# One pool of buffers for attention and experts, and an expert's first weights loaded ahead of the last batch

## The chip, the cores and the metric

The kernel runs on one core of a Trainium2 chip. The metric is the time of one execution on the device in microseconds (us). TensorE (PE) multiplies matrices, VectorE (DVE) and ScalarE (ACT) work on what it leaves in PSUM and on data in SBUF, GpSimd (POOL) copies and issues the indirect transfers, SyncE (SP) issues the plain transfers.

## What is computed

Linear attention without a softmax, with a normalised output, and behind it a mixture of eight experts, of which each token takes the one with the highest score:

```python
kv  = einsum('bhsd,bhse->bhde', k, v)          # b, h = 8, 8; s = 576; d = 64
out = einsum('bhsd,bhde->bhse', q, kv)
out = out / sqrt(mean(out * out, -1) + 1e-6) * g_norm
x   = out, as [4608 tokens, 512]
expert = argmax(x @ w_gate)                    # 8 experts
p      = softmax(x @ w_gate)[expert]
y[token] = p * (relu(x[token] @ w1[expert]) @ w2[expert])   # 512 -> 1024 -> 512
```

Inputs and output are fp32. A token's expert depends on the data, so rows have to be sorted by expert while the kernel runs.

## The kernel before

**Attention** goes in 36 steps of 128 tokens (the loop at L704). In step s TensorE multiplies the turned queries with K^T V of their batch (`x_mm`, L358), turns the queries of step s + 2 (`x_qt`, L342), and works on K^T V of a coming batch (`kv_mm`, L291; `kv_copy`, `kv_t`, `kv_gate`, L305 to L326). ScalarE squares the result (L389) and makes the reciprocal root (L398, L400), VectorE sums (L394) and writes scaled rows `xg` (L408), from which routing (`Route`) finds each row's expert and rank. GpSimd scatters each block of 128 rows into a scratch in DRAM, sorted by expert (L591). What else happens in a step hangs in three lists, `mid`, `late` and `last`: `at(last, 21, f)` puts f behind the work of step 21.

**Weights** are loaded in fp32 and cast to fp16. `stage1` and `stage2` (L146, L154) issue a 2 MB load of W1 and one of W2 on SP's queue; `half1(engine, kk)` (L173) casts a quarter of W1, on ScalarE (L178) or VectorE (L180), `half2` (L184) a quarter of W2. For expert 0 both loads are hung at step 21, behind the load of batch 7's k, v and q (hung at step 20), and W1's quarters are cast at steps 27 to 30, by ScalarE and VectorE in turn.

**The first three tiles of experts 0 and 1** (`Early`, j0 and j1) are worked on out of attention's pools. j1's three products with W2 are at L784 to L790: `two` is the product (L505), `done` scales it into `ys` (L512) and issues its store (`put`, L214).

**The experts' stage** has pools of its own, opened at L793 when attention's are closed, and nine jobs: the rest of experts 0 and 1 (two tiles of 128 rows each), experts 2 to 7 (five tiles each) and one tile of left-over rows. A job is:

- `flip` (L855): four transposes turn a tile of 128 rows into the PSUM tile `xp`, VectorE copies it to `xt` (L868) and makes the row numbers (L208, `place_rows`). The flips of job n + 1 stand between the blocks of job n.
- `one` (L873): a block. Four matmuls make 128 of the 1024 hidden values for the job's columns (256, or 320 in each of two halves, or 128) in the PSUM tile `hp`, and ScalarE's ReLU writes them to `ht` (L888). A job has 8 blocks, or 16 where it has two halves.
- `two` (L892): eight matmuls make the output rows of a tile in `yp`; VectorE scales them into `ys` (L900) and GpSimd stores them (L214).

[...]the stage gives two to `xp`, three to `hp` and three to `yp`, each bank a tile of its own. Between the blocks VectorE casts W1 of the next job (L180), between the products ScalarE casts W2 (L192), and GpSimd gathers the rows of the job after next (L197, `next_row`). The five gathers for expert 2 and the first two flips of job 0 stand ahead of the loop (L944 to L947). In job 2, behind the second product, VectorE makes the table of left-over rows (`left_over_table`, L798 to L844).

The order on every engine is the written one within a `manual_schedule` (all five engines are under it); there are two of them, one for attention and one for the experts' stage. A tile framework places tiles: a pool hands out `bufs` buffers for each tag in turn, and a new tile of a tag waits for those who used the buffer before; it adds the semaphores.

Of the kernel before, what the change touches and what calls it, by code (L numbers as in the profile page):

```python
# [11 lines left out]
F32 = mybir.dt.float32  # L12
F16 = mybir.dt.float16
# [15 lines left out]
def kernel(  # L29
# [16 lines left out]
    E = 8  # L46
# [181 lines left out]
    with (  # L228
        tc.manual_schedule(engines=by_hand),
        tc.tile_pool(name="pattn", bufs=1) as PA,  # L230
        tc.tile_pool(name="psattn", bufs=1, space=bass.MemoryType.PSUM) as PSA,
    ):
# [374 lines left out]
        def at(where, s, fn, *args):  # L607
            where[s].append(lambda: fn(*args))
# [53 lines left out]
        at(last, 21, W[0].stage1)  # L662
        at(last, 21, W[0].stage2)
        at(last, 30, W[1].stage_in, PA)
        for kk in range(4):
            at(last, 27 + kk, W[0].half1, nc.vector if kk % 2 else nc.scalar, kk)
# [117 lines left out]
        yp0 = PSA.tile([128, D], F32, tag="qtp", bufs=1, name="yp")  # L784
        j1.two(0, yp0)
        j1.done(0, yp0)
        yp = PSA.tile([128, 2, D], F32, tag="kvp", bufs=1, name="yp")
        for t in (1, 2):
            j1.two(t, yp[:, t - 1, :])
            j1.done(t, yp[:, t - 1, :])  # L790


    with (  # L793
        tc.tile_pool(name="pffn", bufs=1) as PF,
        tc.tile_pool(name="psffn", bufs=1, space=bass.MemoryType.PSUM) as PSF,
    ):

        def left_over_table():  # L798

            ovr = PF.tile([128, 8], F32, tag="ovr")  # L800
            nc.vector.tensor_sub(ovr, cnt, dlt)
            nc.vector.tensor_scalar(ovr, ovr, float(CAP), 0.0, op0=ALU.subtract, op1=ALU.max)
            thr = PF.tile([128, 8, 32], F32, tag="thr")
# [4 lines left out]
            ov = PF.tile([128, 8], F32, tag="ov")  # L808
            nc.vector.reduce_sum(ov, thr, axis=AXX)
            oi = PF.tile([128, 8], F32, tag="oi")  # L810
            zero8 = PF.tile([128, 8], F32, tag="zero8")
            nc.vector.memset(zero8, 0.0)
            nc.vector.tensor_tensor_scan(oi, ov, zero8, 0.0, op0=ALU.add, op1=ALU.add)
            cm = PF.tile([128, 32, 8], F32, tag="thr")
            nc.vector.tensor_tensor(cm, _bc(oi, 1, 32), _bc(tcol, 2, 8), op=ALU.is_le)
            te = PF.tile([128, 32], F32, tag="te")
            nc.vector.reduce_sum(te, cm, axis=AXX)
            nc.vector.tensor_tensor(cm, cm, _bc(ov, 1, 32), op=ALU.mult)
            tk = PF.tile([128, 32], F32, tag="tk")
# [3 lines left out]
            e8 = PF.tile([128, 8], F32, tag="e8")  # L823
            nc.vector.tensor_scalar(e8, eoff, 1.0 / N, None, op0=ALU.mult)
            nc.vector.tensor_tensor(cm, _bc(te, 2, 8), _bc(e8, 1, 32), op=ALU.is_equal)
            cd = PF.tile([128, 32, 8], F32, tag="cd")
            nc.vector.tensor_tensor(cd, cm, _bc(dlt, 1, 32), op=ALU.mult)
            td = PF.tile([128, 32], F32, tag="td")
# [16 lines left out]

        class Job:


            def __init__(self, xe, w, okm, bgm, views):
                self.xe, self.w, self.okm, self.bgm, self.views = xe, w, okm, bgm, views  # L850
                self.nt = nt = len(xe)
                self.cols = nt * 128
                self.halves = 2 if self.cols > 512 else 1

            def flip(self, t):  # L855

                nt, xe = self.nt, self.xe
                if t == 0:
                    self.xt = PF.tile(
                        [128, 4, nt * 128], F16, tag=f"xt{nt}", bufs=2, name="xt"  # L860
                    )
                    self.idx = PF.tile([128, nt], I32, tag=f"idx{nt}", bufs=3, name="idx")
                xp = PSF.tile([128, 4, 128], F16, tag="xp", bufs=2, name="xp")
                for c in range(4):
                    nc.tensor.transpose(  # L865
                        xp[:, c, :], xe[t][:, c * 128:(c + 1) * 128], ident16
                    )
                nc.vector.tensor_copy(self.xt[:, :, t * 128:(t + 1) * 128], xp)  # L868
                place_rows(
                    self.idx[:, t:t + 1], xe[t], self.okm[:, t:t + 1], self.bgm[:, t:t + 1]  # L870
                )

            def one(self, ws, f):  # L873
                if ws == 0 and f == 0:
                    self.ht = PF.tile(
                        [128, 8, self.cols], F16, tag=f"ht{self.nt}", bufs=2, name="ht"
                    )
                wd = self.cols // self.halves
                hp = PSF.tile([128, wd], F32, tag="hp", bufs=3, name="hp")
                for kk in range(4):  # L880
                    nc.tensor.matmul(  # L881
                        hp,
                        self.w.w1[:, kk, f * 128:(f + 1) * 128],
                        self.xt[:, kk, ws * wd:(ws + 1) * wd],
                        start=(kk == 0),
                        stop=(kk == 3),
                    )
                nc.scalar.activation(  # L888
                    self.ht[:, f, ws * wd:(ws + 1) * wd], hp, ACTF.Relu
                )  # L890

            def two(self, t):  # L892
                yp = PSF.tile([128, D], F32, tag="yp", bufs=3, name="yp")
                for f in range(8):
                    nc.tensor.matmul(  # L895
                        yp, self.ht[:, f, t * 128:(t + 1) * 128], self.w.w2[:, f, :],
                        start=(f == 0), stop=(f == 7),
                    )
                ys = PF.tile([128, D], F32, tag="ys", bufs=8, name="ys")
# [5 lines left out]
        def left_over(t, t0, view):  # L905
# [5 lines left out]
            okm = PF.tile([128, 1], F32, tag="okm", bufs=2, name="okm")  # L911
            nc.vector.tensor_tensor(okm, pcol, nvf[:, bass.ds(t, 1)], op=ALU.is_lt)
            bgm = PF.tile([128, 1], F32, tag="bgm", bufs=2, name="bgm")
            nc.vector.tensor_scalar(bgm, okm, -BIG, BIG, op0=ALU.mult, op1=ALU.add)
            gi = PF.tile([128, 1], I32, tag="gi", bufs=2, name="gi")
# [7 lines left out]
        with tc.manual_schedule(engines=by_hand):  # L923
            jobs = []
            for n, e in enumerate(order):
                if e == "left":
                    jobs.append(None)
                    continue
                t0 = AT if n < 2 else 0
                x0 = 2 * AT + 2 * n if n < 2 else (10, 0, 5)[(n - 2) % 3]  # L930
                jobs.append(Job(
                    xe_bufs[x0:x0 + CT - t0], W[n], valid[:, e, t0:CT], bigm[:, e, t0:CT],
                    out_views[e * CT + t0:(e + 1) * CT],
                ))

            tick2 = PF.tile([128, 1], F16, tag="tick2")

            def next_row(n, t, job, ws, f):

                c = ws * (job.cols // job.halves)  # L940
                nc.gpsimd.tensor_copy(tick2, job.ht[:, f, c:c + 1])  # L941
                gather(jobs[n].xe[t], rowi[:, order[n], t:t + 1])

            for t in range(CT):  # L944
                gather(jobs[2].xe[t], rowi[:, 2, t:t + 1])
            for t in range(2):
                jobs[0].flip(t)  # L947

            for n in range(len(order)):
                job = jobs[n]  # L950
                if n == 4:
                    jobs[E] = left_over(0, 3 * CT, out_views[E * CT])
                    W[E] = jobs[E].w
                nxt = jobs[n + 1] if n + 1 < len(order) else None
                flips = list(range(nxt.nt)) if nxt is not None else []
                coming = list(range(CT)) if 0 < n < len(order) - 3 else []
                for ws in range(job.halves):
                    for f in range(8):
                        job.one(ws, f)
                        step = 8 * ws + f  # L960
                        if coming and (step % 3 == 0 if n > 1 else f < 5):
                            next_row(n + 2, coming.pop(0), job, ws, f)
                        if ws == job.halves - 1 and f >= 2 and flips:
                            nxt.flip(flips.pop(0))
                        if n > 0 and ws == 0 and f % 2 == 1 and nxt is not None:
                            W[n + 1].half1(nc.vector, f // 2)
                            if f == 7 and n + 2 < len(order):
                                W[n + 2].stage1()
                for kk in range(max(job.nt, 4)):
                    if kk < job.nt:  # L970
                        job.two(kk)
                    if n > 0 and kk < 4 and nxt is not None:
                        W[n + 1].half2(kk)
                        if kk == 3 and n + 2 < len(order):
                            W[n + 2].stage2()
                    if n == 2 and kk == 1:
                        left_over_table()

        nov = nc.values_load(tabi[0:1, 1, 7:8], min_val=0, max_val=NOV)
        with tc.If(nov > 1):  # L980
            with tc.For_i(1, nov) as t:
                job = left_over(t, 3 * CT, out_views[E * CT + 1])
                job.w.stage1()
                job.w.stage2()
                for kk in range(4):
                    job.w.half1(nc.vector, kk)
                    job.w.half2(kk)
                job.flip(0)
                for f in range(8):
                    job.one(0, f)  # L990
                job.two(0)
# [28 lines left out]
```

## Time and profile before

| | us |
|---|---|
| median of 3 runs | 304.49 (304.31 to 304.61) |
| the profiled execution | 330.63 |
| its span, first to last instruction | 328.7 |
| TensorE busy | 276.4 (84%) |
| ScalarE busy | 165.8 (50%) |
| VectorE busy | 157.9 (48%) |
| GpSimd busy | 164.3 (50%) |
| mean granted clock of TensorE | 0.935 of full |

Times in the profile come from one execution with the profiler on, which took 26.1 us more than the median. A row of the timeline is: start, duration, engine, line, operation, output and input with their shapes, how often, and in brackets how long the engine had been idle before it and what ended that. A row of the groups is: line, engine, operation, how often | busy us, mean ns of one | idle us before it, and what ended most of it. "issue" is a wait whose end the profile doesn't show. TensorE's matmuls are pipelined, and their ends are modelled.

### The profile page before, as it was taken

To read this page: it belongs to the slowest core of one execution; us is meant where nothing else is said; L and a number is where in the kernel's file an instruction comes from. 1 tells how busy PE (TensorE), PEld (TensorE's weight loads), DVE (VectorE), ACT (ScalarE), POOL (GpSimd) and SP (SyncE) were. 2 spreads that over 40 slices of the span, in tenths; PEclk is the share of its full clock that TensorE was granted. 3 is DMA by queue.
4 is the path that set the end of the run, shared out by engine and by line. 5 is a ranking of instruction groups with operands and counts; after the bars stand their busy time and mean duration, and the time that the engine had idled before them with its cause. 6 is when DMAs were issued, how large, how long until landed. Compare 5 with 4: busy or idle time off the path is not lost. (4 is left out here: it accounts for less than half of the span.)

```text
span 328.7 us, 7210 instructions
## 1 busy us (share of the span) xinstructions
PE 276.4 (84%) x2832; PEld 191.5 (58%) x2832; DVE 157.9 (48%) x424; ACT 165.8 (50%) x353; POOL 164.3 (50%) x238
## 2 busy tenths in 40 slices
PE   8897989979996967258952999799979999999992
PEld 3586877868885856224521665456446474665651
DVE  0034856844784747524321280787453354546130
ACT  1245766643764656427800356455434466473831
POOL 9511253764365663742773088327685484305051
PEclk9999999985999898769995899999997999999999
DMA  7999878949599767320695029997779597987330
GB/s 283 373 391 389 323 259 313 397 121 394 169 401 398 299 205 277 99 76 26 223 379 221 2 82 350 390 352 272 302 257 402 154 368 290 312 322 254 150 123 33
DMA packets 34883, 85.73 MB, mean 261 GB/s; under 512 B 3868, under 2 KB 4125, under 8 KB 34848
## 3 DMA queue, kind: packets, MB, share of 16 engines
q1 hardware_dynamic: 26592, 65.10, 54.9%
q0 software_dynamic: 6976, 18.96, 15.8%
q10 hardware_dynamic: 1280, 1.20, 1.1%
q8 instruction: 23, 0.38, 0.5%
q14 instruction: 12, 0.10, 0.1%
HBM read 71.71 MB, written 15.50 MB: 265 GB/s over the span
## 5 line engine op out<-in xcount | busy, mean ns | idle before, releaser
L888 ACT ACTIVATE ht<-hp 128x320 f16<-128x320 f32 (+2 forms) x120 | 49.1, 419 | 81.2 <-PE hp L881 70.4
L881 PE MATMUL hp<-xt,w1e 128*128 128x320 f16 (+2 forms) x480 | 72.2, 299 | 11.8 <-DVE xt L868 5.9
L214 POOL DMA_INDIRECT out_dram<-ys,idx x41 | 42.7, 1042 | 71.3 <-DVE ys L900 61.7
L881 PEld LDWEIGHTS <-w1e 128*128 128x128 f16 x480 | 45.7, 100 | 29.0 <-issue 7.4
L895 PE MATMUL yp<-w2e,ht 128*128 128x512 f16 x280 | 61.9, 379 | 0.0
L368 PE MATMUL op<-kvs,qts 128*128 128x144 f32 (+1 forms) x320 | 50.3, 315 | 3.2 <-DVE xg L408 1.9
L591 POOL DMA_INDIRECT xs_scratch<-xg,sli x36 | 35.4, 983 | 22.8 <-issue 22.2
L895 PEld LDWEIGHTS <-ht 128*128 128x128 f16 x280 | 27.3, 98 | 31.4
L368 PEld LDWEIGHTS op<-kvs,qts 128*128 128x128 f32 (+1 forms) x320 | 41.3, 193 | 6.8 <-DVE xg L408 2.3
L900 DVE TENSOR_SCALAR ys<-yp,xe 128x512 f32<-128x512 f32 x35 | 26.0, 750 | 39.9 <-PE yp L895 38.7
L197 POOL DMA_INDIRECT xe<-xs_scratch,rowi x34 | 35.7, 1049 | 9.4 <-issue 6.0
L394 DVE TENSOR_REDUCE ms<-sq 128x8 f32<-128x512 f32 x36 | 24.6, 684 | 22.0 <-ACT sq L389 18.4
L389 ACT ACTIVATE sq<-op 128x512 f32<-128x512 f32 x36 | 21.5, 596 | 25.6 <-PE op L368 22.6
L192 ACT CAST w2e<-ws 128x1024 f16<-128x1024 f32 x32 | 31.2, 1041 | 1.5 <-DMA ws<-in_moe_w_dram 1.5
L868 DVE COPY xt<-xp 128x512 f16<-128x512 f16 x35 | 14.7, 421 | 34.4 <-PE xp L865 21.1
L346 PE MATMUL qtp<-cf,qp 128*128 128x128 f32 x144 | 24.2, 293 | 1.5 <-POOL qp L282 1.5
L299 PE MATMUL kvp<-v,k 64*64 64x64 f32 x1152 | 24.4, 227 | 1.3 <-DMA v<-in_v_dram 0.7
L180 DVE TENSOR_SCALAR w1e<-ws,g 128x1024 f16<-128x1024 f32 x31 | 21.9, 755 | 6.8 <-DMA ws<-in_moe_w_dram 6.8
L408 DVE TENSOR_TENSOR xg<-op,rinv 128x512 f16<-128x512 f32 x36 | 24.5, 681 | 0.0
L299 PEld LDWEIGHTS kvp<-v,k 64*64 64x64 f32 x1152 | 20.3, 138 | 7.0 <-issue 7.0
L353 ACT COPY qts<-qtp 128x512 f32<-128x512 f32 x36 | 21.1, 585 | 6.4 <-PE qtp L346 6.3
L282 POOL COPY qp<-q 128x512 f32<-128x512 f32 x32 | 19.6, 626 | 9.3 <-DMA q<-in_q_dram 9.2
(115 smaller groups left out, 275.9 us busy)
## 6 DMA issues: line engine op xcount, KB each, us to landing
ws<-in_moe_w_dram SPq DMA_DIRECT2D x16, 2048.0 KB
q<-in_q_dram SPq DMA_DIRECT2D x8, 1152.0 KB
k<-in_k_dram SPq DMA_DIRECT2D x7, 1152.0 KB
v<-in_v_dram SPq DMA_DIRECT2D x7, 1152.0 KB
ws<-in_moe_w_dram SPq DMA_DIRECT2D x4, 1024.0 KB
k<-in_k_dram SPq DMA_DIRECT2D x2, 576.0 KB
v<-in_v_dram ACTq DMA_DIRECT2D x2, 576.0 KB
out_dram<-ys,idx POOLq DMA_INDIRECT x41
```

The lines of the kernel that those rows point to most:

```text
L192: copy(self.w2[:, 2 * kk:2 * kk + 2, :], self.s2[:, 2 * kk:2 * kk + 2, :])
L197: return nc.gpsimd.indirect_dma_start(out=xe.bitcast(I32), out_offset=None, in_=xs.ap() if src is None else src, in_offset=IndirectOffsetO ...
L214: nc.gpsimd.indirect_dma_start(out=view, out_offset=IndirectOffsetOnAxis(ap=idx, axis=0), in_=ys, in_offset=None, bounds_check=N - 1, oob_ ...
L299: nc.tensor.matmul(kvst[b][64 * ip:64 * ip + 64, c, 64 * i2:64 * i2 + 64], ld["k", b][ps, i, cs], ld["v", b][ps, i, cs], start=(j == 0), s ...
L368: nc.tensor.matmul(op[ts, c, 144 * i2:144 * i2 + 144], qts[s][:, 2 * i2 + c, ts], kvs[:, 2 * c + i2, :], start=True, stop=True,)
L394: nc.vector.reduce_sum(ms, sq, axis=AXX)
L408: nc.vector.tensor_tensor(xg[:, r, 0:512].rearrange("p (i h c n) -> p c i h n", c=2, i=2, h=2), ox, _bc(r4, 4, 64), op=ALU.mult,)
L591: put_xs = nc.gpsimd.indirect_dma_start(out=xs_views[9 * self.P + self.g0 + t], out_offset=IndirectOffsetOnAxis(ap=self.sli[:, t:t + 1], a ...
L881: nc.tensor.matmul(hp, self.w.w1[:, kk, f * 128:(f + 1) * 128], self.xt[:, kk, ws * wd:(ws + 1) * wd], start=(kk == 0), stop=(kk == 3),)
L888: nc.scalar.activation(self.ht[:, f, ws * wd:(ws + 1) * wd], hp, ACTF.Relu)
L895: nc.tensor.matmul(yp, self.ht[:, f, t * 128:(t + 1) * 128], self.w.w2[:, f, :], start=(f == 0), stop=(f == 7),)
L900: nc.vector.tensor_scalar(ys, yp, self.xe[t][:, 514:516].bitcast(F32), None, op0=ALU.mult)
```

## The change

Attention's pools, SBUF (`PA`) and PSUM (`PSA`), stay open to the end, and the experts' stage takes its buffers from them by attention's tags, in one `manual_schedule`:

- PSUM: `xp` becomes half of a tile of two banks (tag kvp, one buffer), for two flips in a row; `hp` becomes half of a tile of two banks (tag op, two buffers), for two blocks in a row; `yp` takes two tiles of one bank in turn (qtp, misc).
- SBUF: `xt` takes the buffers of k, `ht` is split into two tiles of four blocks in those of v and q, `ys` goes round seven buffers (five of qp, two of sq) where it had eight.
- j1's three products use the same two `yp` tiles, and the first two flips of job 0 stand ahead of the third. The five gathers for expert 2 stand behind j1's stores.
- Expert 0's W1 load is hung at step 19, which is ahead of the load of batch 7 on SP's queue; its four casts are all ScalarE's, at steps 22, 24, 26 and 28.

```diff
-    with (
-        tc.manual_schedule(engines=by_hand),
-        tc.tile_pool(name="pattn", bufs=1) as PA,
-        tc.tile_pool(name="psattn", bufs=1, space=bass.MemoryType.PSUM) as PSA,
-    ):
+    PA = ctx.enter_context(tc.tile_pool(name="pa", bufs=1))
+    PSA = ctx.enter_context(tc.tile_pool(name="psa", bufs=1, space=bass.MemoryType.PSUM))
+
+    with tc.manual_schedule(engines=by_hand):
...
-        at(last, 21, W[0].stage1)
+        at(last, 19, W[0].stage1)
         at(last, 21, W[0].stage2)
         at(last, 30, W[1].stage_in, PA)
         for kk in range(4):
-            at(last, 27 + kk, W[0].half1, nc.vector if kk % 2 else nc.scalar, kk)
+            at(last, 22 + 2 * kk, W[0].half1, nc.scalar, kk)
...
-        yp0 = PSA.tile([128, D], F32, tag="qtp", bufs=1, name="yp")
-        j1.two(0, yp0)
-        j1.done(0, yp0)
-        yp = PSA.tile([128, 2, D], F32, tag="kvp", bufs=1, name="yp")
-        for t in (1, 2):
-            j1.two(t, yp[:, t - 1, :])
-            j1.done(t, yp[:, t - 1, :])
-    with (
-        tc.tile_pool(name="pffn", bufs=1) as PF,
-        tc.tile_pool(name="psffn", bufs=1, space=bass.MemoryType.PSUM) as PSF,
-    ):
...
+        banks = ["qtp", "misc"]
+        spare = ["qp", "sq", "qp", "qp", "sq", "qp", "qp"]
...
             def flip(self, t):
-                    self.xt = PF.tile(
-                        [128, 4, nt * 128], F16, tag=f"xt{nt}", bufs=2, name="xt"
-                    )
+                    self.xt = PA.tile([128, 4, nt * 128], F16, tag="k", bufs=2, name="xt")
-                xp = PSF.tile([128, 4, 128], F16, tag="xp", bufs=2, name="xp")
+                if t % 2 == 0:
+                    self.xp = PSA.tile([128, 2, 8, 128], F16, tag="kvp", bufs=1, name="xp")
+                xp = self.xp[:, t % 2, 0:4, :]
...
             def one(self, ws, f):
-                if ws == 0 and f == 0:
-                    self.ht = PF.tile(
-                        [128, 8, self.cols], F16, tag=f"ht{self.nt}", bufs=2, name="ht"
-                    )
+                if ws == 0 and f % 4 == 0:
+                    self.ht.append(PA.tile(
+                        [128, 4, self.cols], F16, tag="vq"[f // 4], bufs=2 + f // 4,
+                        name="ht",
+                    ))
-                hp = PSF.tile([128, wd], F32, tag="hp", bufs=3, name="hp")
+                if f % 2 == 0:
+                    self.hp = PSA.tile([128, 2, 512], F32, tag="op", bufs=2, name="hp")
+                hp = self.hp[:, f % 2, 0:wd]
...
             def two(self, t):
-                yp = PSF.tile([128, D], F32, tag="yp", bufs=3, name="yp")
+                banks.reverse()
+                yp = PSA.tile([128, D], F32, tag=banks[0], bufs=1, name="yp")
...
-                ys = PF.tile([128, D], F32, tag="ys", bufs=8, name="ys")
+                spare.append(spare.pop(0))
+                ys = PA.tile(
+                    [128, D], F32, tag=spare[0], bufs=5 if spare[0] == "qp" else 2, name="ys"
+                )
...
-            for t in range(CT):
-                gather(jobs[2].xe[t], rowi[:, 2, t:t + 1])
-            for t in range(2):
-                jobs[0].flip(t)
+        for t in range(AT):
+            if t == 2:
+                for u in range(2):
+                    jobs[0].flip(u)
+            banks.reverse()
+            yp = PSA.tile([128, D], F32, tag=banks[0], bufs=1, name="yp")
+            j1.two(t, yp)
+            j1.done(t, yp)
+        for t in range(CT):
+            gather(jobs[2].xe[t], rowi[:, 2, t:t + 1])
```

The table of left-over rows and the job of a left-over tile take their small tiles from the same pool; what they compute is the same.

## The prediction

> **What bounds the kernel now.** I read the groups of instructions first, then the timeline at three places: where attention's buffers hand over to the experts' (155 to 185 us), inside one expert late in the run (286 to 309), and around the table of left-over rows (210 to 226); last, steps 22 to 32 of attention.
>
> The groups say who paces the experts:
>
> ```profile
> L888 ACT ACTIVATE ht<-hp 128x320 f16<-128x320 f32 (+2 forms) x120 | 49.1, 419 | 81.2 <-PE hp L881 70.4
> L881 PE MATMUL hp<-xt,w1e 128*128 128x320 f16 (+2 forms) x480 | 72.2, 299 | 11.8 <-DVE xt L868 5.9
> ```
>
> ScalarE waited 70.4 us for TensorE in front of its ReLUs, TensorE almost nothing. TensorE is the bound of the experts' stage. Now the handover:
>
> ```profile
> 168.00 0.75 DVE L512 TENSOR_SCALAR ys<-yp,xe 128x512 f32<-128x512 f32 x1 [2.01 <-PE yp L505]
> ...
> 168.81 1.89 PE L505 MATMUL yp<-w2e,early 128*128 128x512 f16 x8 [1.88 <-issue]
> ...
> 178.78 0.42 DVE L868 COPY xt<-xp 128x512 f16<-128x512 f16 x1 [5.68 <-DMA out_dram<-ys,idx]
> ...
> 179.72 2.74 PE L881 MATMUL hp<-xt,w1e 128*128 128x256 f16 x12 [5.91 <-DVE xt L868]
> ```
>
> Two waits are seen. The first copy into the new pool (L868) waits until the last store of expert 1 from attention's pool has landed (issued by GpSimd at 175.12; in the chain of waits its landing takes 3.03 us). TensorE stands until 179.72. And the third product of expert 1 (168.81) starts 0.06 us after VectorE has read the second (168.00 + 0.75 = 168.75): they lie in two halves of one tile, yp [128, 2, 512] (L787), each a bank of its own, and still the later write waits for the read of the other half. So the program's dependencies here go by the tile, not by the half. Keep this in mind.
>
> Inside an expert:
>
> ```profile
> 288.49 0.71 PE L881 MATMUL hp<-xt,w1e 128*128 128x320 f16 x4
> ...
> 289.24 0.44 ACT L888 ACTIVATE ht<-hp 128x320 f16<-128x320 f32 x1 [0.33 <-PE hp L881]
> ...
> 300.74 6.14 PE L881 MATMUL hp<-xt,w1e 128*128 128x320 f16 x44
> 301.56 5.79 ACT L888 ACTIVATE ht<-hp 128x320 f16<-128x320 f32 x11 [5.05 <-PE hp L881]
> ```
>
> Eleven blocks of four matmuls without a gap: weight loads of 6.02 us for them, 0.546 us a block. Its ReLU starts 0.75 us after the block's first matmul and takes 0.44. With three hp tiles (L879) nobody waits for it.
>
> **What the Trainium skill says.** "TensorE: Matmul & The Clock Gate", section "Single matmul latency": warm, (398 + N)/2.4 ns, which is 299 ns for N = 320. The row of L881 has 299 ns on average: agreed; so a result is complete some 0.2 us after the next matmul could have started, and 0.546 + 0.2 is the 0.75 above. The same page, section "The HAM clock gate": after an idle window of about 3.4 us the clock goes to half. The trace agrees: granted clock 0.50 in 175 to 180 and 0.62 in 180 to 185, behind the handover; it also fell to 0.5 after a stretch of 3.41 us (245.24 to 248.65) with TensorE busy for 1.51, and did not after one with 2.04 (204.28 to 207.69). "PSUM — Partial Sum Buffer", section "PSUM bank collisions raise a hardware error": what must be kept apart is a bank and quadrant. The two halves of a pair are different banks, so the chip would not need the wait seen at 168.81; the program makes it.
>
> **The change part by part.** The profiled execution took 330.63 us (span 328.7), the median of the runs shown is 304.49: 26.1 less. All terms are sums in the profiled execution's microseconds, and I carry the difference to the median unscaled.
>
> *1. One pool: the handover goes.* In the built program after, the last product of expert 1 stands behind the two flips of the next job and in a tile of its own, so neither the 0.06-after-the-read wait nor the wait for the stores is left. On GpSimd's queue the five gathers for expert 2 (L197, about 1.31 us apart) now stand behind expert 1's three stores, and not among them. TensorE then goes on: two products until about 167.1, eight transposes (L865, x8: 0.67), the third product (1.73), to 169.5; the copies follow the read that ends at 168.75, two of 0.42 and an idx of 0.21 between, so about 169.8. Against 179.72: **-9.9**. What is late next would be the gathers for expert 2: stores at 165.9, 167.7 and about 170.2, gathers to about 177.9, landed by about 181; first needed by a flip at about 181. Covered, 0 to +1.
>
> *2. Blocks in pairs (hp, two blocks to a tile).* In the built program the first matmul of every second block waits for a ScalarE semaphore, and its value is reached by the ReLU of the first block of the same tile. It is the wait by tile from above, now 60 times. For 320 columns: ReLU starts at 0.75, ends at 1.19, 0.05 to TensorE (as at 243.99 to 244.03), so the second block starts 1.24 after the first and not 0.546: **+0.70 a pair** (1.79 against 1.09). For 256 columns: 189.09 to 189.73 is 0.64, +0.39 +0.05 = 1.08 against 0.44: +0.64. Where a flip (four transposes, 0.22) stands between the two blocks, it uses 0.22 of it: three pairs in a job whose successor has five tiles.
> Jobs 4, 5, 6: 8 x 0.70 - 0.66 = 4.94 each, 14.8. Job 7 (one flip): 5.4. Job 0: 3.97 without any wait (8 blocks of 0.44, two flips), +2.56 -0.22 = 6.3, against the 5.9 it took at half clock behind the handover: +0.4. Job 1: 4.63 + 2.56 - 0.66 = 6.5 against 5.5: +1.0. Job 2: it took 13.36 (198.06 to 211.42) where 9.8 is due, since its flips waited behind VectorE's W1 cast, which waited for its DMA until 205.6 (the chain of waits has it); 9.8 + 4.94 = 14.7, so +1.4, and +0.4 because ScalarE's W2 casts end 1.1 us after its first block starts. Job 3: 14.7 against 11.07: +3.7. The last job (128 columns) waits already: +0.7. Sum: **+27.8**.
>
> *3. Flips in pairs (xp) likewise.* Each flip now waits for the copy of the one before (0.42 + 0.42 + 0.06 = 0.90 after its start); two flips are over 1.0 apart once the pairs wait: 0. Without that cover 0.13 for two flips of each job, 1.7.
>
> *4. Two yp tiles for three.* Ordinarily free: the read ends about 0.8 us after its product and the next takes 1.73. Not in job 2:
>
> ```profile
> 211.25 8.80 PE L895 MATMUL yp<-w2e,ht 128*128 128x512 f16 x40
> ...
> 214.91 0.75 DVE L900 TENSOR_SCALAR ys<-yp,xe 128x512 f32<-128x512 f32 x1 [0.98 <-PE yp L895]
> 215.57 0.16 DVE L801 TENSOR_TENSOR ovr<-cnt,dlt 128x8 f32<-128x8 f32 x1
> ...
> 222.40 2.06 DVE L900 TENSOR_SCALAR ys<-yp,xe 128x512 f32<-128x512 f32 x3
> ```
>
> The table holds VectorE from 215.57 to 222.40. The fifth product needs the tile of the third, read at 222.40 + 0.75 = 223.15; TensorE would be there at 211.42 + 4 x 1.726 = 218.32. **+4.9** (3 to 5). Job 3's blocks are queued behind it.
>
> *5. ys in seven buffers for eight, ht, xt, idx in attention's buffers.* Reuse lies a job or more back, 18 us: 0.
>
> *6. W1 of expert 0.* All four casts go to ScalarE at steps 22, 24, 26, 28. Gone is the one at step 29, which held the copy that TensorE waits for:
>
> ```profile
> 118.41 1.13 ACT L178 ACTIVATE w1e<-ws,g 128x1024 f16<-128x1024 f32 x1
> ...
> 120.20 1.07 PE L323 MATMUL kgp<-gw,kvt 128*128 128x16 f32 x8 [1.12 <-ACT w1e L178]
> ```
>
> -1.0; and VectorE's at 124.35 (0.75), behind which TensorE waited 0.69 for xg (127.26): -0.6. VectorE's other, at 113.66, was followed by an idle VectorE: 0. Added: ScalarE idled 0.62 before step 23's square and 0.85 before step 25's, so 1.13 there delays them by about 0.5, which the two op tiles absorb but for the K^T V copy of batch 6: +0.4. On SP's queue the 2 MB load moves past k, v and q of batch 7. It follows the q load issued at 71.41; with the 3.5 MB ahead of it, 5.6 MB at about 370 GB/s (slices of 8 us reached 373 to 401) land at about 88; its first cast is due at 92.6. Batch 7's loads, issued from 85.84, come up to 5 us later and are first used at 108. Covered; if the cover fails by the steps being faster without the profiler, ScalarE stands 1 to 3 us. Taken: **-1.2** (-2.5 to +2).
>
> Sum: -9.9 + 27.8 + 4.9 - 1.2 = +21.6. Span 350.3, profiled 352.2, **median 326.1**.
>
> **The rivals.** *A, the likeliest:* as above. Its own range: 0.60 to 0.85 a pair is -6 to +9, the rest -3 to +3: 317 to 337. *B, the waits cool the clock:* the pairs leave TensorE busy for about 1.3 of 1.79 us, 70%; the trace held full clock at 60% and lost it at 44%. If it fell in half of the windows, a pair at half clock is 1.07 + 0.2 + 0.44 + 0.05 + 1.07 = 2.83, so 0.52 more on average, 48 times: 351. *C, faster:* the wait by tile costs little, as TensorE would come late to the second block anyway, and the handover decides. The net of +21.6 falls by 0.6 for every 0.01 us a pair, so it is nought at 0.34 a pair; at 0.2, with job 2's old wait left standing, it gives about 299. For it: in jobs 2 and 3 TensorE stood 3.6 and 1.2 us anyway. Against it: the ReLU's 0.44 alone is over that. *D, the change doesn't reach the handover* (a dependency by buffer names keeps the store's landing in it): 336; against it, the built program has no such wait.
>
> **How the numbers follow.** A 0.76, B 0.10, C 0.06, D 0.08. The range 316 to 339 takes in A and D and leaves out B, C and A's edges, 0.2. This kernel's measurement tells 0.2% (0.6 us) from no change. Faster 0.06, same 0.01, slower 0.93.
>
> **What would show it.** Right: second blocks in one tile start about 1.2 us after the first; ReLU waits for TensorE and TensorE for the ReLU in turn; jobs 5 and 6 about 23.4 us long instead of 18.4; no gap at the handover; the fifth product of job 2 late by 5. Wrong: blocks 0.55 apart throughout (C), or a granted clock of 0.5 in jobs 4 to 7 (B).

## The result, and the profile after

The changed kernel takes **333.45 us** in the median of four runs (331.80 to 334.61), the kernel before beside it 304.55: a ratio of 1.094 (95% interval 1.089 to 1.099), so 28.9 us slower. The forecast was 326.1, 21.6 slower. A median here counts every execution of a kernel, a ratio and its interval only those in its usual, faster state, so a ratio is not always the quotient of the two medians beside it. The profiled execution of the kernel before that the forecast was costed from took 330.63 us. That is about what the kernel takes on one of the chips used below (330.19 in the median, 303 to 305 on the others); on which chip it was taken is not on record. The comparisons of stages here use a new profile of the kernel before, of 303.46 us.

The groups of the changed kernel come first. ReLUs and blocks now wait for each other: TensorE waits 24.9 us for ReLUs, where before it waited for none to speak of.

```profile
L882 ACT ACTIVATE ht<-hp 128x320 f16<-128x320 f32 (+2 forms) x120 | 50.2, 419 | 100.5 <-PE hp L875 97.0
L875 PE MATMUL hp<-xt,w1e 128*128 128x320 f16 (+2 forms) x480 | 74.8, 291 | 24.9 <-ACT ht L882 24.9
```

Its timeline at the handover:

```profile
151.29 0.75 DVE L511 TENSOR_SCALAR ys<-yp,xe 128x512 f32<-128x512 f32 x1 [0.97 <-PE yp L504]
151.95 0.41 DVE L859 COPY xt<-xp 128x512 f16<-128x512 f16 x1
...
152.64 1.89 PE L504 MATMUL yp<-w2e,early 128*128 128x512 f16 x8
...
154.37 0.60 PE L875 MATMUL hp<-xt,w1e 128*128 128x256 f16 x4
```

No wait for a store is left between the last product of expert 1 and the first block; the block begins when the product's matmuls are through. In the new profile of the kernel before, TensorE stood there (what waited for what, us in total, times, longest):

```profile
PE hp L881 <- DVE xt L868: 8.4, 1, 8.4
```

Inside expert 5 of the changed kernel:

```profile
251.66 0.71 PE L875 MATMUL hp<-xt,w1e 128*128 128x320 f16 x4
...
252.49 0.44 ACT L882 ACTIVATE ht<-hp 128x320 f16<-128x320 f32 x1 [5.05 <-PE hp L875]
...
252.98 1.25 PE L875 MATMUL hp<-xt,w1e 128*128 128x320 f16 x8 [0.61 <-ACT ht L882]
```

The second block (252.98) starts 0.05 us after the ReLU of the first ends (252.93), 1.32 after the first; the third, in the other tile, follows it at once, and the fourth waits again. At the table of left-over rows:

```profile
193.40 0.16 DVE L788 TENSOR_TENSOR ovr<-cnt,dlt 128x8 f32<-128x8 f32 x1
...
200.23 1.40 DVE L898 TENSOR_SCALAR ys<-yp,xe 128x512 f32<-128x512 f32 x2
201.03 3.57 PE L890 MATMUL yp<-w2e,ht 128*128 128x512 f16 x8 [4.88 <-DVE ys L898]
204.39 1.27 PE L875 MATMUL hp<-xt,w1e 128*128 128x320 f16 x4
```

The fifth product stands 4.88 us for the tile that VectorE reads behind the table. It then takes 3.36 us (201.03 to 204.39, at a granted clock of 0.50) where the others take 1.73.

Now stage by stage. The columns are the stretch, its length, the busy time of TensorE, of its weight loads, of VectorE, ScalarE and GpSimd (with the number of instructions), the granted clock, the DMA share and its rate in GB/s. First the kernel before, in the new profile. The stretches: expert 0's first blocks to the start of job 0 (the handover in it), jobs 0 and 1, job 2, job 3, jobs 4 to 6, job 7.

```profile
124.29:160.81 36.52, 24.79 (x136) 12.49 (x136) 11.65 (x40) 14.96 (x21) 23.55 (x24) 0.87 0.61 218
160.81:178.56 17.75, 17.75 (x125) 12.26 (x126) 8.63 (x22) 9.00 (x20) 7.26 (x10) 0.87 0.14 41
178.56:201.58 23.02, 20.26 (x126) 12.20 (x125) 11.45 (x31) 11.67 (x21) 13.18 (x17) 0.93 0.98 360
201.58:220.17 18.59, 18.59 (x126) 11.26 (x124) 12.62 (x31) 10.76 (x20) 12.48 (x16) 1.00 0.90 302
220.17:275.50 55.33, 55.33 (x374) 33.86 (x372) 28.18 (x60) 32.28 (x60) 30.30 (x37) 1.00 0.91 324
275.50:293.05 17.55, 17.55 (x110) 10.40 (x108) 6.99 (x11) 10.76 (x20) 4.68 (x5) 1.00 0.46 169
```

The same stretches of the changed kernel:

```profile
127.32:154.37 27.05, 24.45 (x137) 12.63 (x137) 11.11 (x39) 14.97 (x21) 17.77 (x18) 0.94 0.57 200
154.37:174.38 20.01, 17.21 (x125) 11.06 (x124) 9.46 (x22) 9.00 (x20) 15.20 (x18) 1.00 0.55 185
174.38:204.39 30.01, 21.80 (x125) 11.76 (x124) 15.41 (x43) 11.57 (x21) 12.19 (x16) 0.92 0.92 333
204.39:228.32 23.93, 20.60 (x125) 11.60 (x124) 9.20 (x19) 10.76 (x20) 11.54 (x15) 0.96 0.51 166
228.32:298.35 70.03, 59.98 (x374) 34.10 (x373) 28.16 (x60) 32.28 (x60) 29.80 (x37) 1.00 0.70 250
298.35:321.24 22.89, 18.83 (x109) 10.40 (x108) 6.99 (x11) 10.76 (x20) 4.68 (x5) 1.00 0.34 129
```

TensorE has the same matmuls to do. From job 3 on the kernel before left it no idle time (length and TensorE's busy time agree), while 10.05 of 70.03 us in jobs 4 to 6 are now idle, at a granted clock of 1.00. Busy times run to the modelled ends of the matmuls, so they hide a part of the wait: the three jobs are 14.70 us longer. The handover gives 36.52 - 27.05 = 9.47 us, everything after it takes more. And the first stretch begins 3.03 us later. Attention's steps 22 and 23 show where that comes from:

```profile
84.74 0.69 DVE L407 TENSOR_TENSOR xg<-op,rinv 128x512 f16<-128x512 f32 x1
...
87.25 1.15 ACT L178 ACTIVATE w1e<-ws,g 128x1024 f16<-128x1024 f32 x1 [3.03 <-DMA ws<-in_moe_w_dram]
88.31 0.58 ACT L388 ACTIVATE sq<-op 128x512 f32<-128x512 f32 x1
...
90.35 0.68 DVE L407 TENSOR_TENSOR xg<-op,rinv 128x512 f16<-128x512 f32 x1
```

ScalarE stands 3.03 us for expert 0's W1 to land, the square of step 23 stands behind it, and the scaled rows of the two steps (L407) are 5.61 us apart. In the kernel before they are 2.54 apart:

```profile
84.89 0.69 DVE L408 TENSOR_TENSOR xg<-op,rinv 128x512 f16<-128x512 f32 x1
...
87.43 0.68 DVE L408 TENSOR_TENSOR xg<-op,rinv 128x512 f16<-128x512 f32 x1
```

### The profile page after: what moved, and what is told of

Same layout as the page of the kernel before. It is cut to its first block, busy times and chain, and to the rows that moved or that the text cites. A ratio compares the mean times of both kernels' runs of the same rounds, so it can differ in the third digit from the quotient of the medians.

```text
span 331.9 us, 7210 instructions
## 1 busy us (share of the span) xinstructions
PE 277.8 (84%) x2832; PEld 185.9 (56%) x2832; DVE 158.3 (48%) x422; ACT 168.6 (51%) x355; POOL 164.3 (50%) x238
## 4 chain that ended last, share of the span: by engine, by line
PE 45%; DMA 21%; ACT 11%; issue 10%; DVE 8%; POOL 2%; SPq 1%; POOLq 1%; ACTq 0%; DVEq 0%
PE hp L875 14%; DMA ws<-in_moe_w_dram 8%; PE op L367 8%; PE yp L890 8%; DMA out_dram<-ys,idx 8%; ACT ht L882 5%; PE kvp L298 5%; PE qtp L345 3%; DMA k<-in_k_dram 2%; PE hp L493 2%; POOL out_dram L214 2%; DVE ms L393 2%; DMA g<-in_g_norm_dram 2%; ACT w2e L192 1%; PE yp L504 1%
## 5 line engine op out<-in xcount | busy, mean ns | idle before, releaser
L882 ACT ACTIVATE ht<-hp 128x320 f16<-128x320 f32 (+2 forms) x120 | 50.2, 419 | 100.5 <-PE hp L875 97.0
L875 PE MATMUL hp<-xt,w1e 128*128 128x320 f16 (+2 forms) x480 | 74.8, 291 | 24.9 <-ACT ht L882 24.9
L890 PE MATMUL yp<-w2e,ht 128*128 128x512 f16 x280 | 63.7, 386 | 4.9 <-DVE ys L898 4.9
L367 PE MATMUL op<-kvs,qts 128*128 128x144 f32 (+1 forms) x320 | 47.3, 303 | 3.5 <-DVE xg L407 2.5
L197 POOL DMA_INDIRECT xe<-xs_scratch,rowi x34 | 36.4, 1072 | 13.1 <-issue 5.2
L590 POOL DMA_INDIRECT xs_scratch<-xg,sli x36 | 35.4, 983 | 14.7 <-issue 14.4
L367 PEld LDWEIGHTS op<-kvs,qts 128*128 128x128 f32 (+1 forms) x320 | 38.5, 183 | 7.0 <-DVE xg L407 3.0
L859 DVE COPY xt<-xp 128x512 f16<-128x512 f16 x35 | 14.8, 424 | 44.9 <-PE xp L856 43.8
L281 POOL COPY qp<-q 128x512 f32<-128x512 f32 x32 | 19.2, 616 | 11.5 <-DMA q<-in_q_dram 11.4
L407 DVE TENSOR_TENSOR xg<-op,rinv 128x512 f16<-128x512 f32 x36 | 24.5, 681 | 0.0
L345 PE MATMUL qtp<-cf,qp 128*128 128x128 f32 x144 | 23.3, 285 | 1.0 <-POOL qp L281 0.8
L180 DVE TENSOR_SCALAR w1e<-ws,g 128x1024 f16<-128x1024 f32 x29 | 20.4, 755 | 5.9 <-DMA ws<-in_moe_w_dram 5.9
## 6 DMA issues: line engine op xcount, KB each, us to landing
ws<-in_moe_w_dram SPq DMA_DIRECT2D x16, 2048.0 KB, 10.3
v<-in_v_dram SPq DMA_DIRECT2D x7, 1152.0 KB, 13.7
```

Of the source, the lines that this page charges most:

```text
L197: return nc.gpsimd.indirect_dma_start(out=xe.bitcast(I32), out_offset=None, in_=xs.ap() if src is None else src, in_offset=IndirectOffsetO ...
L345: nc.tensor.transpose(qtp[:, c, i2, :], qp[s][:, c, 2 * i2:2 * i2 + 2, :], ident)
L367: nc.tensor.matmul(op[ts, c, 144 * i2:144 * i2 + 144], qts[s][:, 2 * i2 + c, ts], kvs[:, 2 * c + i2, :], start=True, stop=True,)
L590: put_xs = nc.gpsimd.indirect_dma_start(out=xs_views[9 * self.P + self.g0 + t], out_offset=IndirectOffsetOnAxis(ap=self.sli[:, t:t + 1], a ...
L875: nc.tensor.matmul(hp, self.w.w1[:, kk, f * 128:(f + 1) * 128], self.xt[:, kk, ws * wd:(ws + 1) * wd], start=(kk == 0), stop=(kk == 3),)
L882: nc.scalar.activation(self.ht[f // 4][:, f % 4, ws * wd:(ws + 1) * wd], hp, ACTF.Relu)
```

## The experiments

Each is timed beside the kernel before on its chip; the twelve fall on three chips, four on each, where the kernel before took 303.71, 330.19 and 304.74 us (27 runs each on the second and third, 11 on the first).

**The kernel before again.** Unchanged.

> The kernel before, unchanged, once more under the profiler. My theory: the profiled execution of before that I costed from held stalls of TensorE that its timed runs don't have (it took 26.1 us more than the median), so a new profile near 304.5 us shows the stages at their usual length: expert 1's first two products to the start of job 0, the handover, again about 10 us of which TensorE stands 6, and jobs 4 to 6 about 18.4 us each. Rival: the profiler itself slows the kernel before, and the new profile takes about 330 us again.

Its profiled execution took 303.46 us. Job 0 starts 36.52 us after expert 0's first block, TensorE standing 8.40 of it for VectorE's first copy, where 6 were expected; jobs 4 to 6 take 18.44 each, as expected. The rival falls: with the profiler on, the kernel takes what it takes without. But the theory's reason doesn't hold either, as the second chip showed: there the timed runs of the kernel before take 330.19 too.

**One block to an hp tile.**

```diff
-                if f % 2 == 0:
-                    self.hp = PSA.tile([128, 2, 512], F32, tag="op", bufs=2, name="hp")
-                hp = self.hp[:, f % 2, 0:wd]
+                self.hp = PSA.tile([128, 2, 512], F32, tag="op", bufs=2, name="hp")
+                hp = self.hp[:, 0, 0:wd]
```

> The changed kernel with one block to a tile of hp: the same two tiles, and the second bank of each left empty, so only two blocks are in flight where there were four. My theory (a block waits for the ReLU of whatever was last written into its tile): block k + 2 waits for ReLU k, which ends 1.24 us after block k's start, so blocks of 320 columns come 0.62 apart and not 1.77 a pair; 0.53 a pair less at 320 columns (48 pairs) and 0.39 at 256 (8 pairs) is 28.5, less some 2 that the flips had hidden: 333.45 falls to about 307 (305 to 310). Rival (the experts' stage is slow because too few blocks are in flight, three banks made into two tiles): halving what is in flight makes it slower, or changes nothing: 333 to 345.

312.30 us, 1.0276 of before (1.0234 to 1.0319), against 1.094: with half as many blocks in flight it is some 20 us faster. So the number of blocks in flight is not what the pairs lose by; they lose by sharing a tile. In the first half of job 5 blocks now start 0.62 us apart on average, as the theory said, and jobs 4 to 6 need 11.13 us for blocks: 9.81 before, 14.71 changed. The time stops short of 307, though. The theory had counted 4.2 us for the eight pairs of job 2, but that job takes 14.71 for 14.69: it stays as long as its wait for the W1 load makes it. And expert 0's first block came 1.6 us later here than in the changed kernel's profile (128.90 for 127.32). A small cost shows in the second half of job 5:

```profile
250.12 0.39 PE L856 MATMUL xp<-ch,xe 128*128 128x128 f16 x4
...
250.34 0.71 PE L874 MATMUL hp<-xt,w1e 128*128 128x320 f16 x4
250.54 0.42 DVE L859 COPY xt<-xp 128x512 f16<-128x512 f16 x1 [3.55 <-PE xp L856]
...
251.02 0.38 PE L856 MATMUL xp<-ch,xe 128*128 128x128 f16 x4
```

The next flip waits for the copy of the last (250.96), though it writes the other half of xp: a flip and a block come every 0.90 us. Before, they took 0.22 + 0.55 = 0.77. This is the price that the forecast put under cover of the pairs' wait; it shows once that is gone. Of the 1.32 us that job 5's blocks still take more than before, it makes 0.5; the eleven blocks ahead of the flips, at 0.62 us for 0.55, make 0.8. The table still cost 6.6.

**The table earlier.**

```diff
                     job.one(ws, f)
+                    if n == 2 and ws == 0 and f == 0:
+                        left_over_table()
...
-                if n == 2 and kk == 1:
-                    left_over_table()
```

> The changed kernel with the table of left-over rows made behind the first block of job 2, ahead of the W1 casts there that wait for their load in any case, and not behind that job's second product. My theory (the fifth product waits for the tile of the third, whose scaling stands behind the table): 4.9 us less, 328.5 (327.5 to 330). Rival (the table's time is only moved: the casts and flips behind it come as late as the product did): 332 to 334.

329.24 us, 1.0824 (1.0781 to 1.0866). In its profile job 2's products take 8.63 us for 15.32, and job 3's blocks 14.68 for 15.30; job 2's own blocks take 14.86 for 14.69. So 7.1 us net came back, the 4.9 of the wait and what the half clock behind it had cost; the rival falls. In the time it is 3.5 to 5 less (1.0824 against 1.094 and 1.0994 of the changed kernel). In this profile ScalarE stood longer for W1, 4.2 us, and expert 0's first block came 2.8 later, which takes a part of the gain back.

**Expert 0's W1 as before, in the changed kernel.**

```diff
-        at(last, 19, W[0].stage1)
+        at(last, 21, W[0].stage1)
...
-            at(last, 22 + 2 * kk, W[0].half1, nc.scalar, kk)
+            at(last, 27 + kk, W[0].half1, nc.vector if kk % 2 else nc.scalar, kk)
```

> The changed kernel with expert 0's W1 as before: load hung at step 21, casts at steps 27 to 30 by ScalarE and VectorE in turn. My theory after the result (the first cast stands for a load that lands some 3 us too late, and ScalarE's square of step 23 stands behind it): 3 us come back and the 1.2 that the new places were to save are lost, about 331.7 (330.5 to 332.7). Rival, as I predicted (the load is covered, the new places save 1.2): 334.6 (334 to 336).

332.11 us, 1.0955 (1.0904 to 1.1005): in time this tells nothing, since the interval reaches into the ranges of both theories. The profile does: expert 0's first block starts at 124.29, as in the kernel before, for 127.32, and what follows takes as long as in the changed kernel.

**One ReLU for a pair.** The changed kernel, with the edit below; a gather that an even block had paced is paced by the odd block behind it.

```diff
-                nc.scalar.activation(
-                    self.ht[f // 4][:, f % 4, ws * wd:(ws + 1) * wd], hp, ACTF.Relu
-                )
+                if f % 2 == 1:
+                    nc.scalar.activation(
+                        self.ht[f // 4][:, f % 4 - 1:f % 4 + 1, ws * wd:(ws + 1) * wd],
+                        self.hp[:, :, 0:wd], ACTF.Relu,
+                    )
...
```

> The changed kernel with one ReLU for both blocks of an hp tile in place of one for each (GpSimd's gathers that were paced by an even block are paced by the odd one behind it). Theory (the loss lies in the dependency by tile, which a ReLU between two blocks of one tile turns into a wait): the pair's blocks run on, the ReLU of 640 columns ends some 2.0 us after the pair's start, and its tile is wanted again at 2.18: jobs 4 to 6 fall from 14.7 to about 10.3 us of blocks (9.8, and the flips, which still wait for each other's copies, 0.14 each). That is about 25 us less of the 29.4 that the blocks lost: about 308 (305 to 311). Rival (two tiles of hp are too few whatever shares them; ScalarE's longer ReLU comes later): no better than one block to a tile, 312 or more.

On the second chip, 334.69 us beside 330.19 of the kernel before: 1.0114 (1.0056 to 1.0171), 4.5 us slower where 308 for 303.7 meant 4.3. TensorE's wait for ReLUs is 1.3 us in all. Job 7, with one flip, is back at 8.92 us of blocks, as before. Jobs 4 to 6 take 11.7, 11.4 and 10.3, where 10.3 was expected. On this chip the experts' stage of the kernel before isn't even either: in the profile of the run with the W1 part alone, below, its jobs 4 to 6 take 14.5, 10.5 and 9.8. The rival falls: two tiles are enough if their halves are freed together.

**All four repaired, one pool.** Beside three of the edits above (the table earlier, W1 as before, one ReLU for a pair), flips go two at a time behind an odd block, with one copy:

```diff
-                nc.vector.tensor_copy(self.xt[:, :, t * 128:(t + 1) * 128], xp)
+                if t % 2 == 1 or t == nt - 1:
+                    t0 = t - t % 2
+                    nc.vector.tensor_copy(
+                        self.xt[:, :, t0 * 128:(t + 1) * 128].rearrange(
+                            "p k (u n) -> p k u n", n=128
+                        ),
+                        self.xp[:, 0:t + 1 - t0, 0:4, :].rearrange("p u k n -> p k u n"),
+                    )
...
-                    if ws == job.halves - 1 and f >= 2 and flips:
-                        nxt.flip(flips.pop(0))
+                    if ws == job.halves - 1 and f >= 3 and f % 2 == 1:
+                        for _ in range(min(2, len(flips))):
+                            nxt.flip(flips.pop(0))
```

> The changed kernel with all of what I hold for its losses taken out and the one pool kept: one ReLU for each pair of blocks, flips in pairs behind the odd blocks with one copy for both, the table of left-over rows ahead of job 2's W1 casts, expert 0's W1 loaded and cast as in the kernel before. Theory (the handover's 9.5 us are won, and everything lost comes from these four places): 303.7 - 9.5 = about 294, and up to 4 more if the W1 loads that job 2 waits for come no earlier than now (292 to 299). Rival (the one pool has a cost of its own that these places only showed, the longer reuse of its buffers, for one): 303 or more.

On the second chip 321.49, 0.9655 of before (0.9589 to 0.9722). Since 294 was meant for a chip on which the kernel before takes 303.7, it was run again:

> The kernel with all four losses taken out and the one pool kept, as in the run on the slower chip, where it was 0.9655 of the kernel before. Theory (the handover's 9.5 us are won, nothing else): 0.968 of the kernel before (0.962 to 0.978), 294 us where that takes 303.7. Rival (the gain on the slower chip came from that chip's longer landings of the stores, which the handover waits for): 0.98 or more on a chip where the kernel before takes 304.

**291.04 us beside 304.74: 0.9531 (0.9491 to 0.957)**, more than the theory's range. The rival falls. The windows of this profile, the same stretches:

```profile
125.93:152.39 26.46, 24.81 (x136) 12.75 (x136) 10.89 (x38) 14.97 (x21) 17.10 (x17) 0.92 0.53 182
152.39:168.12 15.73, 15.69 (x125) 10.95 (x124) 8.87 (x19) 7.86 (x12) 12.00 (x14) 1.00 0.66 233
...
189.87:208.31 18.44, 18.44 (x125) 11.30 (x124) 8.90 (x17) 9.39 (x12) 12.06 (x16) 1.00 0.98 343
208.31:263.64 55.33, 55.33 (x373) 33.90 (x372) 27.17 (x54) 28.18 (x36) 29.85 (x37) 1.00 0.89 317
```

From job 3 on TensorE is as full as before. What I had left out is the second row: jobs 0 and 1 take 15.73 for 17.75. With no long gap ahead of them the clock is 1.00 and not 0.87, and job 0's blocks take 3.94 for 6.12. Handover and clock together are 10.1 + 2.0. The handover's gain belongs to the one pool together with the new order in it (two flips ahead of the third product, the gathers behind the stores); the two were not tried apart. The groups show what one ReLU for a pair does:

```profile
L890 ACT ACTIVATE ht<-hp 128x640 f16<-128x640 f32 (+2 forms) x60 | 40.1, 668 | 67.9 <-PE hp L882 67.9
...
L882 PE MATMUL hp<-xt,w1e 128*128 128x320 f16 (+2 forms) x480 | 64.8, 290 | 0.1
```

Sixty ReLUs in 40.1 us for 120 in 50.2, and blocks that wait 0.1 us.

**The W1 part alone, in the kernel before.** The two edits to W1's load and casts that stand in the diff of the change, and nothing else.

> The kernel before with the W1 part of the change alone: expert 0's W1 load hung at step 19, all four casts on ScalarE at steps 22, 24, 26 and 28. Theory (the first cast stands for the load): attention ends 3 to 6 us later, as in three profiles with these places against two without, so 303.7 becomes about 307.5 (306 to 309.5). Rival, as predicted (covered, 1.2 saved): 302.5.

On the second chip 330.14 beside 330.19: 0.9979 (0.9947 to 1.0012). That looked like the rival's case. But there the first cast came at 90.1 us, when the load had landed, and ScalarE didn't wait for it. So again:

> The kernel before with the W1 part of the change alone, again: on the slower chip it made no difference (0.9979). Theory (attention's steps are late there, so the load has landed when the first cast comes; where steps are at their usual pace the cast stands): on a chip where the kernel before takes 304 us, 3 to 5 us slower; where it takes 330 us, no difference. Rival (the part costs nothing anywhere, and the 3 us between the profiles are scatter): within 1 us on both.

308.78 beside 304.74, 22 and 27 runs: 1.0094 (1.0065 to 1.0123), so 2.9 us slower (2.0 to 3.7), at the low end of the 3 to 5 expected. The rival falls. Whether the part costs anything on a chip goes with whether the load has landed when step 22 ends.

**The pairs alone, in the kernel before.** Its own pools, yp with three tiles, xp with one.

```diff
-                xp = PSF.tile([128, 4, 128], F16, tag="xp", bufs=2, name="xp")
+                xp = PSF.tile([128, 4, 128], F16, tag="xp", bufs=1, name="xp")
...
-                hp = PSF.tile([128, wd], F32, tag="hp", bufs=3, name="hp")
+                if f % 2 == 0:
+                    self.hp = PSF.tile([128, 2, 512], F32, tag="hp", bufs=2, name="hp")
+                hp = self.hp[:, f % 2, 0:wd]
```

> The kernel before, with its two groups of pools, and of the change only the pairs: hp as half of a tile of two banks, two such tiles, and to make room one buffer of xp for two; yp keeps three. Theory (the loss of the blocks is the pairs' alone, and the table's is that of two yp tiles alone): jobs 3 to 6 gain 4.9 us each, job 7 5.3, jobs 1 and 8 2.1 each, about 29 in all, and the products of job 2 stay at 8.6 us: 333 (329 to 336). Rival (the loss needs the one pool, its order of tiles or its buffers): 304 to 312.

On the second chip 357.45 beside 330.19: 1.0824 (1.076 to 1.0887), 27.3 us for the 29 expected. Jobs 4 to 6 take 14.70 us for blocks, as in the changed kernel, and job 2's products 8.63. The first line of its waits of TensorE (what waited for what, us in total, times, longest):

```profile
PE hp L883 <- ACT ht L890: 21.7, 47, 1.3
```

So the pairs make the blocks' loss without the one pool, and the table's loss needs two yp tiles. This run also took one buffer of xp away; what that costs by itself was not tried, but the waits above are for ReLUs.

**The changed kernel again,** beside the last three on the third chip.

> The changed kernel, unchanged, timed beside the three below on one chip, since the chip of the last four runs took 330.19 us for the kernel before, where others took 304. Theory: the losses are counted in waits between engines (29.4 us of blocks, 6.7 at the table, 3 and more at the first W1 cast) less 9.5 at the handover, so the difference to the kernel before stays near 29 us, 27 to 31, on a chip of either kind. Rival (the difference depends on the chip as the times do): under 25 or over 34.

334.57 beside 304.74: 1.0994 (1.0938 to 1.1051), 29.8 us, within the theory's range. ScalarE stood 2.2 us for W1 there. The changed kernel was not run on the second chip, so that the difference is the same on a chip of that kind is not shown.

**Repaired, with the early load and later casts.**

```diff
-        at(last, 21, W[0].stage1)
+        at(last, 19, W[0].stage1)
...
-            at(last, 27 + kk, W[0].half1, nc.vector if kk % 2 else nc.scalar, kk)
+            at(last, 24 + 2 * kk, W[0].half1, nc.scalar, kk)
```

> The repaired kernel of this batch with expert 0's W1 load at step 19, as in the changed kernel, and its four casts on ScalarE two steps later than there, at steps 24, 26, 28 and 30. Theory (the new places lose only through a cast that comes before its load; at step 24 it has landed): 0 to 2 us faster than the repaired kernel beside it, through the casts no longer ahead of what TensorE waits for at step 29. Rival (the load itself does the harm, since batch 7's k, v and q come 5 us later behind it): 2 us or more slower than that kernel.

289.76 us, 0.9509 of before (0.9463 to 0.9555), beside 0.9531 (0.9491 to 0.957): the intervals overlap, so a gain is not shown, but the rival's loss is excluded. Its first cast came at 88.9 us and did not wait.

## Why the prediction came out right, and where it was short

The prediction was right in direction, in the mechanism of the two large losses and in its range; it was short by 7.3 us in time and by 8.7 in the profiles. It stayed in its range because the range was wide: of the terms that are off by more than 1 us, only one, job 2's, errs to the other side. The terms, in us, measured as the difference of the changed kernel's profile to the new one of before:

| step of the prediction | forecast | measured |
|---|---|---|
| 1, handover | -9.9 | -9.5 |
| 2, pairs: job 0, job 1 | +0.4, +1.0 | +0.2, +2.1 |
| 2, job 2's blocks | +1.8 | +0.3 |
| 2, job 3 | +3.7 | +5.3 |
| 2, jobs 4 to 6; job 7 | +14.8; +5.4 | +14.7; +5.3 |
| 2, last job | +0.7 | +2.1 |
| 4, two yp tiles at the table | +4.9 | +6.7 |
| 6, expert 0's W1 | -1.2 | +3.0 |
| sum (of the unrounded terms) | +21.6 | +30.3 |

*Step 1* was right in its mechanism (a store's landing that the first copy waits for, and a product that waits for the other half's read) and to 0.4 us in size. The gathers, named as next late, stayed covered.

*Step 2* was right: +0.70 a pair was forecast; 1.77 us a pair measured in jobs 4 to 6, against 1.09, is 0.68. One block to a tile and one ReLU to a pair each took the wait away, and the pairs alone brought it into the kernel before. Its terms for jobs 1, 3 and the last were too small mainly for one reason: they were taken against a profile in which these jobs of the kernel before took 5.5, 11.37 and 3.79 us for blocks (the 11.07 in the forecast is a misreading of the second); in the new one they take 4.72, 9.96 and 1.94. Job 2's term was too large: its blocks took 14.39 us before in the new profile, behind the W1 load, and 14.69 now, so the pairs' wait lies beside that wait there. And 0.6 us of job 3 is a cold clock behind the table (14.68 us when the table was moved). One support was weaker than it was said to be: the 299 ns of the row of L881 are a mean over three widths, and the ends of matmuls are modelled (320 columns alone show 303 ns there, 299 in the repaired kernel). What carries the 0.2 us is the ReLU that starts 0.75 us after the block.

*Step 4*: the wait was forecast at 4.9 and is 4.88. Left out was what follows it: the product behind it runs at half clock, 3.36 for 1.73 us. I had used this very effect for the handover, and not asked it of a wait that I was adding. Of this, "The HAM clock gate" in the Trainium skill's "TensorE: Matmul & The Clock Gate" speaks (half clock after some 3.4 us idle); the 4.88 us fit it. The fall that the forecast read behind 245.24 to 248.65 goes beyond that sentence, since TensorE was busy for 1.51 us of it. The 58 waits of the pairs, 0.43 us each on average, did not bring the clock down, as the windows' 1.00 for jobs 4 to 6 shows. So B is out.

*Step 6* failed, at the word "Covered": +3.0 for the -1.2 forecast. The cover rested on when W1's load can start, how long it takes, and when its first cast is due. That the load landed at 87.2, for about 88 forecast, is luck: two errors met in it. Start and due time were read from the profile with the late steps. There step 22 ends at 92.6; at the usual pace it ends at 84.2. There the q load ahead of W1 was issued at 71.41; in the changed kernel's profile it was issued at 67.14, and the forecast's 16.6 us from there would have landed W1 at 83.7. So at the usual pace the cover was 0.5 us and not 4.6. And the load took 20.1 us from there, 3.5 more than counted:

```profile
67.14:87.20 20.06, 19.12 (x339) 16.82 (x339) 13.91 (x37) 11.86 (x31) 12.86 (x24) 1.00 1.02 363
```

At 363 GB/s that is 7.3 MB, where the forecast counted 5.6. Rows that GpSimd scattered and, issued from 77.49 on, batch 7's k and v were under way in it too; that they are what held the load up is argued, not tried. The text named this case, 1 to 3 us, and took the other. The row of step 23 is 2.9 us late against the new profile of before, that of step 25 4.6, and by step 31 it is 3.0 again. So about the saving that I had put down (1.0 and 0.6) came back where the casts are gone from. The wait of 3.0 I had not taken, and the 1.6 lost between steps 24 and 25, where the second cast stands ahead of a square and a K^T V copy, I had put at 0.4 (that the cast is its cause is argued, not tried).

*Steps 3 and 5*: 0 in the changed kernel, as said. Step 3's price without its cover is 0.13 a flip, as forecast; it shows in the one-block kernel.

*A and C*: A is what came. C needed the pair's wait under 0.34 us; it is 0.68. *D* is out by the handover's timeline.

What stays open: why the second chip takes 26 us more for the kernel before. Profiles from it show waits of ScalarE and TensorE with no end that the trace names, 9.7 us at the longest; the profile that the forecast was costed from has one of 9.0 at the same place. Open too is the scatter of the W1 part: expert 0's first block comes 2.8 us later in one profile with the new places than in another, and 1.6 us later in one with the old places.

## What to carry to other kernels

Two buffers made as halves of one tile are one buffer to whoever tracks dependencies by the tile: count tiles, not banks, or write and free the halves together, with one instruction that reads both. The saving that came with the shared pools (12 us in the profiles here, 13.7 in the medians, once the losses were repaired) is real, but read first what each tile count costs at the worst place for it, not in the usual round: a table of 6.8 us between two reads. And ask of each wait that a change adds whether it is long enough to bring the clock down behind it. A due time and a landing are as good as the profile they are read from: check that the profiled execution is near the median before costing a cover of a few us by it, and count everything that shares the DMA with the load.

## What had not been expected of the hardware

The kernel before took 303.71 and 304.74 us on two chips and 330.19 on another, in the median of 11, 27 and 27 runs; one and the same part of the change gives a ratio of 1.0094 on one of the faster chips (1.0065 to 1.0123) and 0.9979 on the slower (0.9947 to 1.0012). A ReLU over two banks, 640 columns, took 0.70 us for 2 x 0.44.
